# Where and on which engine an attention-plus-MLP kernel forms the operands of its seven-product blocks

## The chip, the cores and the metric

The kernel runs on one core of a Trainium2 chip. The metric is the device time of one execution in microseconds (us), as the median of several runs. The core has five engines with a queue each: TensorE (PE: matmuls, and PEld: their weight loads), VectorE (DVE), ScalarE (ACT), GpSimd (POOL) and SyncE (SP), which here issues nearly all DMAs. Each engine takes its instructions in the order of its queue; an instruction that waits holds all behind it on the same engine.

## The reference

Attention over chunks, then a gated MLP on its output:

```
for each chunk c of 32 queries (768 queries, 4 batches, 8 heads of 64):
    keys = 8 memory keys + the chunk with 16 to its left and 8 to its right
    a    = softmax(q_c @ keys.T / 8)
    out  = a @ values
x  = out as 3072 tokens x 512
xn = x / sqrt(mean(x*x) + 1e-6) * rms_g
g, val = xn @ w_gate, xn @ w_val            # 512 x 1536 each
y  = (silu(g) * val) @ w_out                # 1536 x 512
```

## The kernel before

The 3072 tokens are eight blocks of 384. A block's MLP goes over twelve column groups f of 128 of the 1536 columns. Every float32 operand is held as a high part in the matmul format (`fp32r`) and a remainder, and a product is three matmuls: high by high, high by remainder, remainder by high (`PASS`).

**Stages in the order of time.** The first and second block run first, with the loading and splitting of the weights, in an order written out by hand (`ORDER`); of the first block the column groups 5 to 11 are left over. Then `segments` runs the first block's rest, the third block (`blk` 2) and the fourth block (`blk` 3, its column groups in the order 10, 11, 0 to 9). For each column group TensorE does the gate product (`pg`, 12 matmuls), the value product (`pv`, 12) and, one column group behind, the output product (`po`, 9); ScalarE and VectorE do the silu between them (tanh L478, L482, L485, the high part `hh` L173, the remainder `hl` L494). There is one PSUM buffer each for `pg` and `pv`. In the first block VectorE has one multiply more per column group (L473, into the tile `gr`).

The last four blocks run in two pairs (`whole`). There the gate and value products of two blocks and two column groups are formed from seven products in place of eight (`CHAIN`), from sums and differences of weights and of activations, and the parts are added up by VectorE (`products`).

**The weights' sums and differences (the operands of the seven products).** `keep(w, p)` (L766) makes them for one weight matrix (`g` or `v`) and one pair of column groups: SyncE stores the weights that are used as they are (L770, L771) into DRAM; GpSimd adds high part and remainder of both column groups into a tile `ks` (L775, two operations of 128x512) and makes four sums and differences in it (L777, 128x256 each); ScalarE casts the result to the high part in the tile `late["tmp"]` (L779, shown as `qp`); VectorE subtracts to leave the remainder in `ks` (L780); SyncE stores both (L782). `keep_o(f)` (L757) stores the output weights of one column group. There is one tile `ks` and one for the high part. The list `keeping` holds 24 such calls; `visit` (L940) makes the next of them at gaps of the third and fourth block: those of the third whose number does not leave 3 on division by 4, and the odd ones from 1 to 11 of the fourth. A gap is the place behind a `pg` (even numbers) or a `pv` (odd numbers), so a block has 24. Nothing but data and buffers ties these calls to their place: the program's planner orders every engine's queue by a simulated time, and only matmuls are held in program order there.

**Attention.** The attention of the third to eighth block is cut into steps (`late_steps`): "p" transposes, "s" scores and softmax, "o" output, "n" the three parts of the normalization (`late_n`; L348, L349 and L353 are its last operations). `VISITS` says at which gaps of a segment which steps come, `SUPER` does so for the seven-product stage of the first pair. At the end of a block `split_x` (L733) makes high part and remainder of the next block's activations, and the last silu (L747, L748).

**The activations' sums.** `x_first`, `x_second` and `x_rest` make the activations' sums and differences for the seven products by `half` (cast and remainder, L815 and L816) and `minus` (L819), each on 128x768. For the first pair they come behind column groups number 7 and 10 of the fourth block and at its end. The first 30 loads of stored operands (`load(NR)`, L811) are issued behind column group number 7 of the fourth block.

## Time and profile before

| | us |
|---|---|
| median of 3 runs | 707.48 |
| lowest and highest run | 705.79 and 708.33 |
| the profiled execution's own time | 708.44 |
| its span, first to last instruction | 706.7 |
| TensorE busy | 672.8 |
| VectorE busy | 449.5 |
| ScalarE busy | 299.2 |
| GpSimd busy | 75.0 |

Mean granted TensorE clock: 0.983 of full speed. The third block's first gate product starts at about 227 us, the fourth's at 317 and the first seven-product at about 410.

The rows of the trace give a start time or a total in us, the engine and the line, the operation with its output and inputs by their names in the program, their shapes, and how often it stands there. In square brackets or behind an arrow stands how long the engine was idle just before and what it was waiting for. The name of a tile is the name under which its buffer was first made: `qp` is also `late["tmp"]`.

### The profile page before, as it was taken

The page shows a single profiled execution, that of the slowest core. Times are in us where ns is not written, and L with a number is a line of the kernel's source. Part 1 is how long each engine was busy: PE and PEld are TensorE (multiplying, and loading weights), DVE is VectorE, ACT ScalarE, POOL GpSimd, SP SyncE. Part 2 cuts the span into 40 slices and gives each one's busy share as a digit, 9 for nine tenths or more (in the row PEclk, how much of TensorE's full clock was granted, in tenths as well). Part 3 has the DMA queues.
Part 4 walks back from the last instruction along what each step waited for, and adds up shares of the span by engine and source line. Part 5 has one row for each costly group of instructions (what it writes and reads, how often), then busy time and mean ns, then how long its engine had stood idle before and what let it go on. Part 6 is the DMA issues. An engine that isn't in the chain of part 4 may idle for free.

```text
span 706.7 us, 15057 instructions
## 1 busy us (share of the span) xinstructions
PE 672.8 (95%) x6134; PEld 613.5 (87%) x6134; DVE 449.5 (64%) x831; ACT 299.2 (42%) x516; POOL 75.0 (11%) x84
## 2 busy tenths in 40 slices
PE   7899999999886989999999999999999999999997
PEld 6797888999775988799999989989988899999885
DVE  6689988887587543585585967569729254455221
ACT  4597867843333331433324254343424343332112
POOL 0010000034536335300000000000000000000000
PEclk8799999999998999999999999999999999999999
DMA  9659997866642252513319668896733598885002
GB/s 328 266 164 338 313 342 245 268 221 224 223 165 102 93 185 68 182 58 135 105 46 355 256 206 248 298 304 222 251 113 120 165 304 252 254 251 176 0 1 89
DMA packets 79700, 140.18 MB, mean 198 GB/s; under 512 B 7440, under 2 KB 33040, under 8 KB 79632
## 3 DMA queue, kind: packets, MB, share of 16 engines
q1 hardware_dynamic: 77760, 136.08, 58.0%
q10 hardware_dynamic: 1872, 3.15, 1.2%
q8 instruction: 48, 0.79, 0.4%
q14 instruction: 20, 0.16, 0.1%
HBM read 104.60 MB, written 34.60 MB: 197 GB/s over the span
## 4 chain that ended last, share of the span: by engine, by line
PE 65%; DVE 10%; DMA 9%; POOL 7%; ACT 6%; issue 3%; SPq 0%; POOLq 0%; DVEq 0%; ACTq 0%
PE po L915 14%; PE mga L886 7%; PE mva L886 7%; PE pg L464 6%; PE po L514 6%; PE pv L464 6%; POOL ks L777 4%; POOL ks L775 3%; PE mve L886 3%; PE mge L886 3%; DMA ws<-in_moe_w_out_dram 2%; DMA kv<-ks 2%; PE mvc L886 2%; PE mgc L886 2%; DVE ks L780 2%
## 5 line engine op out<-in xcount | busy, mean ns | idle before, releaser
L915 PE MATMUL po<-r,hhs 128*128 128x512 f32 x288 | 90.5, 395 | 0.0
L464 PE MATMUL pv<-xh,wh_v 128*128 128x384 f32 x192 | 66.2, 345 | 7.8 <-ACT xT L316 4.7
L464 PE MATMUL pg<-xh,wh_g 128*128 128x384 f32 x192 | 68.0, 354 | 3.4 <-DVE t L482 2.1
L464 PE MATMUL pv<-xh,wl_v 128*128 128x384 f32 x192 | 65.7, 342 | 0.5 <-DVE wl_v L435 0.5
L464 PE MATMUL pg<-xl,wh_g 128*128 128x384 f32 x192 | 65.9, 343 | 0.0
L464 PE MATMUL pg<-xh,wl_g 128*128 128x384 f32 x192 | 65.8, 342 | 0.0
L464 PE MATMUL pv<-xl,wh_v 128*128 128x384 f32 x192 | 65.5, 341 | 0.0
L514 PE MATMUL po<-wh_o,hh 128*128 128x512 f32 x144 | 58.8, 408 | 6.4 <-ACT hh L747 5.4
L915 PEld LDWEIGHTS po<-r,hhs 128*128 128x128 f32 x288 | 54.1, 188 | 12.3
L514 PE MATMUL po<-wh_o,hl 128*128 128x512 f32 x144 | 58.2, 404 | 1.1 <-DVE hl L494 1.1
L886 PE MATMUL mga<-x,r 128*128 128x384 f32 x288 | 58.4, 338 | 0.0
L886 PE MATMUL mva<-x,r 128*128 128x384 f32 x288 | 58.1, 337 | 0.0
L514 PE MATMUL po<-wl_o,hh 128*128 128x512 f32 x144 | 57.6, 400 | 0.0
L915 PE MATMUL po<-r,hls 128*128 128x512 f32 x144 | 56.8, 395 | 0.0
L897 DVE TENSOR_TENSOR hls<-h,hhs 128x768 fp32r<-128x768 f32 x24 | 22.9, 956 | 45.3 <-ACT hhs L896 45.3
L886 PEld LDWEIGHTS mga<-x,r 128*128 128x128 f32 x288 | 50.4, 188 | 1.0 <-ACT e L858 0.6
L886 PEld LDWEIGHTS mva<-x,r 128*128 128x128 f32 x288 | 50.5, 188 | 0.1
L896 ACT CAST hhs<-h 128x768 fp32r<-128x768 f32 x24 | 20.0, 835 | 68.1 <-PE po L915 64.1
L464 PEld LDWEIGHTS pv<-xh,wh_v 128*128 128x128 f32 x192 | 36.4, 190 | 10.2 <-ACT xT L316 5.6
L173 ACT CAST hh<-t 128x384 fp32r<-128x384 f32 x46 | 23.7, 516 | 46.3 <-PE po L514 22.2
L464 PEld LDWEIGHTS pg<-xh,wh_g 128*128 128x128 f32 x192 | 36.8, 192 | 6.7 <-DVE t L482 2.6
L777 POOL TENSOR_TENSOR ks<-ks 128x256 f32<-128x256 f32 x48 | 37.9, 789 | 2.8
(154 smaller groups left out, 1461.3 us busy)
## 6 DMA issues: line engine op xcount, KB each, us to landing
r<-kg SPq DMA_DIRECT2D x84, 256.0 KB, 3.3
r<-kv SPq DMA_DIRECT2D x84, 256.0 KB, 3.3
r<-ko SPq DMA_DIRECT2D x48, 256.0 KB, 3.1
kv<-in_v_dram SPq DMA_DIRECT2D x24, 384.0 KB, 4.8
kv<-in_k_dram SPq DMA_DIRECT2D x24, 312.0 KB, 3.8
ws<-in_moe_w_gate_dram SPq DMA_DIRECT2D x4, 1024.0 KB, 7.1
ws<-in_moe_w_val_dram SPq DMA_DIRECT2D x4, 1024.0 KB, 7.2
ws<-in_moe_w_out_dram SPq DMA_DIRECT2D x4, 1024.0 KB, 7.1
```

The costliest lines, as they stand in the source:

```text
L173: return nc.scalar.copy(out, in_)
L464: on_pe(nc.tensor.matmul(ps[:, 0:HT], lhsT=weight(a, n, f, kt), rhs=xs[c][:, kt], start=kt == 0 and i == 0, stop=kt == NKT - 1 and i == 2))
L514: on_pe(nc.tensor.matmul(po[i], lhsT=h[a][:, i * P:(i + 1) * P], rhs=weight(c, "o", f), start=f == first and n == 0, stop=f == end and n = ...
L775: nc.gpsimd.tensor_tensor(out=s[:, i:i + 2], in0=h, in1=l, op=ALU.add)
L777: nc.gpsimd.tensor_tensor(out=s[:, o], in0=s[:, a], in1=s[:, b], op=op)
L780: nc.vector.tensor_tensor(out=s.bitcast(F32R), in0=s, in1=h.bitcast(F32), op=ALU.subtract)
L886: on_pe(nc.tensor.matmul(bank[w, b], lhsT=r[:, a, kt], rhs=x[:, c, kt], start=bool(first) and kt == 0 and i == 0, stop=kt == 1 and i == 2, ...
L896: nc.scalar.copy(hh, sup["h", f])
L897: nc.vector.tensor_tensor(out=hl, in0=sup["h", f], in1=hh.bitcast(F32), op=ALU.subtract)
L915: on_pe(nc.tensor.matmul(po[i], lhsT=cur[a][:, i * P:(i + 1) * P], rhs=r[c], start=f == n == 0, stop=f == NF - 1 and n == 2))
```

## The change

The sums and differences of the weights are formed in three steps at set gaps, for each of twelve items (a weight matrix and a pair of column groups), 36 gaps in all: every gap of the third block and the first twelve of the fourth. An item's steps are:

1. VectorE makes the four sums and differences (before: GpSimd), and GpSimd's two sums for the next item are issued;
2. ScalarE casts the high part, in two halves, into a tile of its own (`kh`);
3. VectorE makes the remainder, in two halves, and SyncE issues all of the item's stores, those of one column group of the output weights among them.

GpSimd's two sums for the first item are issued at gap 11 of the first block. `tc.issue_after` holds each step behind what VectorE and ScalarE were given before it. The summed tile has two buffers in turn (`ks` and `late["tmp"]`). `rb0`, `rb1` and `gr` become parts of one tile, whose place is used by `kh` later and by `spare` in the seven-product stage. The attention visits of the fourth block come two gaps sooner, and those in the seven-product stage move. `x_second` comes one column group sooner, and `half` and `minus` work in two halves.

```diff
-          3: {3: "ps", 3.5: "o", 7: "ps", 7.5: "o", 9: "n", 10: "n", 11: "n",
-              13: "ps", 13.5: "o", 17: "ps", 17.5: "o", 19: "n", 20: "n", 21: "n"}}
+          3: {1: "ps", 1.5: "o", 5: "ps", 5.5: "o", 7: "n", 8: "n", 9: "n",
+              11: "ps", 11.5: "o", 15: "ps", 15.5: "o", 17: "n", 18: "n", 19: "n"}}
...
-SUPER = {("A", 1, 2): "p", ("A", 1, 6): "s", ("A", 1, 11): "o", ("A", 2, 11): "p", ("A", 3, 2): "s", ("A", 3, 7): "o",
-         ("A", 3, 12): "n", ("A", 4, 2): "n", ("A", 4, 6): "n", ("A", 4, 10): "p", ("A", 4, 13): "s", ("A", 5, 5): "o",
-         ("B", 1, 5): "p", ("B", 2, 5): "o", ("B", 3, 5): "n", ("B", 4, 2): "n", ("B", 4, 5): "n"}
+SUPER = {("A", 1, 1): "p", ("A", 1, 4): "s", ("A", 2, 0): "o", ("A", 3, 0): "p", ("A", 3, 3): "s", ("A", 4, 0): "o",
+         ("A", 4, 3): "n", ("A", 4, 6): "n", ("A", 5, 1): "n", ("A", 5, 2): "p", ("A", 5, 5): "s", ("B", 0, 2): "o",
+         ("B", 2, 2): "p", ("B", 3, 2): "o", ("B", 4, 2): "n", ("B", 4, 5): "n", ("B", 5, 2): "n"}
...
-        t = p1.tile([P, HT], F32, name="gr", tag="gr")
+        t = gr
...
-    rb = [p1.tile([P, HT], F32, name=f"rb{i}", tag=f"rb{i}") for i in range(2)]
+    spare = p1.tile([P, 3, HT], F32, name="rg", tag="rg")
+    rb, gr = [spare[:, i] for i in range(2)], spare[:, 2]
...
+    def dump(f, w, cols, to):
+        k, i, n = fgroup[f]
         for part in range(2):
-            nc.sync.dma_start(out=t[:, part], in_=weight_all(part, "o", f).bitcast(F32))
+            c = wt[part, w, k].bitcast(F32)[:, i * DM:(i + 1) * DM]
+            nc.sync.dma_start(out=to[:, :, part], in_=c[:, cols].rearrange("p (k f) -> p k f", k=to.shape[1]))
+
+    items, sums = [(p, w) for p in (5, 0, 1, 2, 3, 4) for w in "gv"], {}
+
+    def keep_load(k):
+        p, w = items[k]
+        s = sums[k] = (late["tmp"] if k % 2 else p1.tile([P, 2 * DM], F32, name="ks", tag="wy")).rearrange("p (k f) -> p k f", k=4)
+        for i, f in enumerate(reversed(PAIRS[p])):
+            c, n, _ = fgroup[f]
+            h, l = (wt[part, w, c][:, n * DM:(n + 1) * DM].bitcast(F32).rearrange("p (k f) -> p k f", k=2) for part in range(2))
+            nc.gpsimd.tensor_tensor(out=s[:, 2 * i:2 * i + 2], in0=h, in1=l, op=ALU.add)
+
+    def keep(g):
+        k = g // 3
+        if k >= len(items):
+            return
+        p, w = items[k]
+        s = sums[k]
+        with ExitStack() as behind:
+            for eng in (nc.vector, nc.scalar):
+                behind.enter_context(tc.issue_after(last_of(eng)))
+            if g % 3 == 0:
+                for o, a, b, op in ((1, 0, 1, ALU.add), (0, 2, 0, ALU.subtract), (2, 1, 2, ALU.subtract), (3, 3, 2, ALU.subtract)):
+                    nc.vector.tensor_tensor(out=s[:, o], in0=s[:, a], in1=s[:, b], op=op)
+                if k + 1 < len(items):
+                    keep_load(k + 1)
+            elif g % 3 == 1:
+                sums["h"] = h = p1.tile([P, 3 * HT], F32R, name="kh", tag="rg")[:, 0:2 * DM].rearrange("p (k f) -> p k f", k=4)
+                for i in range(2):
+                    nc.scalar.copy(h[:, 2 * i:2 * i + 2], s[:, 2 * i:2 * i + 2])
+            else:
+                h, t = sums["h"], dram.tile([P, 7, 2, DM // 2], F32, name=f"k{w}{p}")
+                l = s.bitcast(F32R)
+                for i in range(2):
+                    c = slice(2 * i, 2 * i + 2)
+                    nc.vector.tensor_tensor(out=l[:, c], in0=s[:, c], in1=h[:, c].bitcast(F32), op=ALU.subtract)
+                kept[w, p] = t
+                nc.sync.dma_start(out=t[:, 3:7, 0], in_=h.bitcast(F32))
+                behind.enter_context(tc.issue_after(last_of(nc.sync)))
+                nc.sync.dma_start(out=t[:, 3:7, 1], in_=s)
+                fa, fb = PAIRS[p]
+                dump(fa, w, slice(0, DM), t[:, 0:2])
+                dump(fb, w, slice(DM // 2, DM), t[:, 2:3])
+                f = fa if w == "g" else fb
+                kept["o", f] = t = dram.tile([P, 2, DM], F32, name=f"ko{f}")
+                dump(f, "o", slice(0, DM), t.unsqueeze(1))
...
     def half(t, src):
-        nc.scalar.copy(t[:, 0], src)
-        nc.vector.tensor_tensor(out=t[:, 1], in0=src, in1=t[:, 0].bitcast(F32), op=ALU.subtract)
+        for i in range(2):
+            nc.scalar.copy(t[:, 0, i], src[:, i])
+            nc.vector.tensor_tensor(out=t[:, 1, i], in0=src[:, i], in1=t[:, 0, i].bitcast(F32), op=ALU.subtract)
...
         def visit(gap):
+            if blk == 0 and gap == 11:
+                keep_load(0)
+            if blk and gap == int(gap):
+                keep(24 * (blk - 2) + gap)
             for c in VISITS[blk].get(gap, ""):
                 if next(todo) != c:
                     raise AssertionError(gap)
-            if blk == 2 and gap in range(24) and gap % 4 != 3 or blk == 3 and gap in range(1, 12, 2):
-                next(keeping)()
...
-                if blk == 3 and n == 10:
+                if blk == 3 and n == 9:
                     x_second(4)
...
-        sup["e", w, n] = lambda i=i: (p1 if i < 2 else sup["hpool"]).tile([P, HT], F32, name=f"e{i}", tag=f"rb{i}" if i < 2 else f"e{i}")
+        sup["e", w, n] = lambda i=i: sup["spare"][:, i] if i < 2 else sup["hpool"].tile([P, HT], F32, name=f"e{i}", tag=f"e{i}")
```

## The prediction

> **What bounds the kernel now.** I read the page's busy times and chain first, then a table of stretches, then TensorE's pauses one by one, then who held the engine that each pause names.

> ```profile
> PE 672.8 (95%) x6134; PEld 613.5 (87%) x6134; DVE 449.5 (64%) x831; ACT 299.2 (42%) x516; POOL 75.0 (11%) x84
> ...
> HBM read 104.60 MB, written 34.60 MB: 197 GB/s over the span
> ```

> TensorE is busy for 672.8 of 706.7 us: only the 34 us in which it stands, and the time in which it runs at a reduced clock, can be won. The question is how much of both lies where the change works. Columns of the next rows: PE, PEld, DVE, ACT, POOL busy, granted clock, DMA share, GB/s.

> ```profile
> 180.00:223.00 43.00, 32.86 (x364) 28.40 (x356) 34.54 (x63) 15.51 (x30) 19.47 (x20) 0.94 0.50 166
> 223.00:260.00 37.00, 36.95 (x360) 34.04 (x361) 18.30 (x34) 12.38 (x23) 16.97 (x18) 0.93 0.40 136
> 260.00:288.00 28.00, 25.47 (x134) 23.04 (x132) 10.89 (x17) 7.42 (x13) 11.19 (x13) 1.00 0.31 108
> 288.00:317.00 29.00, 27.57 (x314) 23.96 (x313) 21.57 (x47) 10.92 (x23) 5.61 (x6) 1.00 0.32 106
> 317.00:363.50 46.50, 46.50 (x606) 43.27 (x605) 28.18 (x65) 14.83 (x31) 0.00 (x0) 1.00 0.29 97
> 363.50:409.00 45.50, 44.56 (x586) 39.92 (x585) 34.24 (x74) 16.38 (x32) 0.00 (x0) 1.00 0.72 254
> ...
> 196.00:199.00 3.00, 1.75 (x7) 1.75 (x8) 1.47 (x3) 2.14 (x5) 0.00 (x0) 0.79 0.98 297
> 199.00:202.00 3.00, 3.00 (x12) 2.72 (x11) 2.33 (x6) 0.72 (x2) 2.67 (x2) 0.64 0.56 216
> 223.00:226.00 3.00, 2.95 (x7) 2.37 (x8) 2.97 (x4) 1.93 (x4) 1.62 (x2) 0.50 0.27 93
> 226.00:229.00 3.00, 3.00 (x11) 2.71 (x11) 0.09 (x1) 1.26 (x2) 2.84 (x4) 0.59 0.42 157
> ```

> The first stretch is the end of the first block, the third block runs from 223 to 317, the fourth from 317 to 409. Where POOL works (to 297), TensorE pauses; from 317 to 363.5 POOL is idle and TensorE does not pause at all. So the operands, which the code names only in the third and fourth block, are formed much earlier, in the first block's tail. The pauses:

> ```profile
> 184.19 0.44 PE L464 MATMUL pv<-xh,wh_v 128*128 128x384 f32 x1 [1.43 <-ACT xT L316]
> 187.17 0.87 PE L274 MATMUL pT<-ident,pe 128*128 128x128 f32 x6 [0.60 <-DVE gr L473]
> ...
> 197.25 0.44 PE L464 MATMUL pv<-xh,wh_v 128*128 128x384 f32 x1 [1.96 <-ACT xT L316]
> ...
> 208.92 0.50 PE L514 MATMUL po<-wh_o,hl 128*128 128x512 f32 x1 [0.58 <-DVE hl L494]
> 215.71 0.50 PE L514 MATMUL po<-wh_o,hl 128*128 128x512 f32 x1 [0.18 <-DVE hl L494]
> ...
> 223.05 0.79 PE L514 MATMUL po<-wh_o,hh 128*128 128x512 f32 x1 [5.45 <-ACT hh L747]
> ...
> 263.17 0.45 PE L464 MATMUL pg<-xh,wh_g 128*128 128x384 f32 x1 [2.14 <-DVE t L482]
> ...
> 296.73 0.44 PE L464 MATMUL pv<-xh,wh_v 128*128 128x384 f32 x1 [1.28 <-ACT xT L316]
> ...
> 407.22 0.50 PE L514 MATMUL po<-wh_o,hh 128*128 128x512 f32 x1 [0.93 <-ACT hh L173]
> ...
> 477.09 1.33 PE L886 MATMUL mve<-x,r 128*128 128x384 f32 x6 [1.62 <-DVE e L861]
> ```

> None names POOL. The link is one step back, in ScalarE's and VectorE's queues:

> ```profile
> ACT qp L779 <- POOL ks L777: 38.8, 10, 5.9
> ```
> ```profile
> 260.35 1.05 ACT L779 CAST qp<-ks 128x1024 fp32r<-128x1024 f32 x1 [5.32 <-POOL ks L777]
> 261.30 0.48 ACT L478 ACTIVATE t<-pg 128x384 f32<-128x384 f32 x1
> ```
> ```profile
> 211.86 2.77 DVE L348 SCALAR_TENSOR_TENSOR rq<-rq,rt 128x384 f32<-128x384 f32 x2
> 214.55 1.10 DVE L494 TENSOR_TENSOR hl<-t,hh 128x384 fp32r<-128x384 f32 x1
> 215.57 1.08 DVE L349 SCALAR_TENSOR_TENSOR rr<-rq,rr 128x384 f32<-128x384 f32 x1
> 216.69 3.03 DVE L353 SCALAR_TENSOR_TENSOR xT<-xT,rg,rr 128x384 f32<-128x384 f32 x4
> ...
> 220.12 1.21 DVE L780 TENSOR_TENSOR ks<-ks,qp 128x1024 fp32r<-128x1024 f32 x1
> ```
> ```profile
> 358.97 1.14 DVE L348 SCALAR_TENSOR_TENSOR rq<-rq,rt 128x384 f32<-128x384 f32 x2
> 360.15 0.56 DVE L349 SCALAR_TENSOR_TENSOR rr<-rq,rr 128x384 f32<-128x384 f32 x1
> ...
> 361.38 2.20 DVE L353 SCALAR_TENSOR_TENSOR xT<-xT,rg,rr 128x384 f32<-128x384 f32 x4
> ```
> ```profile
> 211.29 2.93 POOL L775 TENSOR_TENSOR ks<-wh_v,wl_v 128x512 f32<-128x512 f32 x2 [5.70 <-DMA kg<-ks]
> ```

> First, the cast L779 stands at the head of ScalarE's queue until POOL has finished its six operations, 38.8 us in ten waits; the tanh behind it (261.30) is late, and TensorE stands 2.14 us at 263.17. Second, VectorE is slower beside POOL: the pair L348 took 2.77 us under POOL's two sums against 1.14 alone, L349 1.08 against 0.56, the four L353 3.03 against 2.20. Third, the cast's remainder L780 stands in the same queue.

> **The change, part by part.**

> *The first block's tail.* All but the first item's sums move behind the third block's start. The pauses from 180 to 223.05 add up to 1.43 + 0.60 + 1.96 + 0.58 + 0.18 + 5.45 = 10.2 us. What of the 5.45 is inherent? Taking out what is named above: 1.63 (L348) + 0.5 (hl, about half of 1.10) + 0.52 (L349) + 0.83 (L353) + 1.21 (L780) = 4.7, which leaves 0.7; more if VectorE has other work to catch up, as this block has one multiply more per column group (L473) than the third. I put 1.0 back, with bounds 0 and 5.45.

> *The clock.* Behind the pauses at 197 and 223 the granted clock fell. Loss: 1.75 x (1 - 0.79) + 3 x (1 - 0.64) = 1.5 us, and 2.95 x (1 - 0.50) + 3 x (1 - 0.59) = 2.7 us; together 4.2, which goes with the pauses. [...] So I charge new pauses up to 2.7 us, and 0.5 as the likeliest.

> *The third block's inside.* 2.14 and 1.28 us are ScalarE's cast waiting for POOL; with the differences made a step earlier by another engine they go: 3.4. The price is VectorE's:

> ```profile
> L780 DVE TENSOR_TENSOR ks<-ks,qp 128x1024 fp32r<-128x1024 f32 x12 | 14.7, 1223 | 25.4 <-ACT qp L779 25.4
> ...
> L321 DVE TENSOR_TENSOR sq<-sq,sq 128x384 f32<-128x384 f32 x18 | 10.0, 558 | 11.0 <-ACT sq L319 10.2
> ```

> No row shows a 128x256 operation on VectorE. From 384 elements (558 ns) to 1024 (1223 ns) it is 1.04 ns an element, so about 425 ns (below the 558 row, above its proportional 372); four, overlapping as the L353 do, about 1.5 us. The remainder, now two halves, stays about 1.25. Each of twelve items thus holds VectorE for 2.75 us where it held it 1.22, and POOL's two sums slow it by 1 us (bounds 0 and the 2.93 of the sums' own length). [...]

> A new wait comes with it: the differences wait at the head of VectorE's queue for POOL's sums, with silu, hl and attention behind them, and TensorE behind those. The sums are issued one item ahead and have a second buffer, so I cost this wait at nothing in the third block. What decides is the landing of the store that frees the buffer, against the length of a gap:

> ```profile
> 304.33 2.11 PE pv L464 x12
> 306.44 2.10 PE po L514 x9
> ```
> ```profile
> 248.11 6.07 DMA kv<-ks
> ...
> 274.29 3.19 DMA kv<-ks
> ```

> A column group (pg like pv, then po) takes 6.3 us, a gap half of that. Four gaps, 12.6 us, lie between the remainder and the differences that reuse its buffer. The remainder (1.25), two issues (about 1), the landing (3.2 alone, 6.1 beside the attention's loads) and the sums (2.9) need 8.4 to 11.3. It holds, with 1.3 us to spare at the worst. ScalarE's cast has one buffer: two gaps, 6.3 us, between the store of its high part and the next cast, against 3.2 to 6.1; it holds too, barely at the worst, and the tanh stands behind it. On SP's queue the stores now lie among the attention's loads, which are needed a visit (four gaps or more) later; the products' first 30 operand loads come behind the fourth block's eighth column group and read items stored by then. Both at nothing.

> *The third block's end.* Seven gaps from 288 to 317 get three remainders and two sets of differences: 6.75, plus 2 for POOL, minus 1.2 for the L780 in it now. VectorE: 21.6 + 7.5 = 29.1 us in 29 - 1.4 = 27.6 us of TensorE's time. It overflows by 1.5, and part of its idle time can't be used (it waits for TensorE's results), so I take a pause of 3 us ahead of the fourth block; bounds 0 and 6.

> *The fourth block's first twelve gaps.* The attention two gaps sooner brings both pairs and the whole normalization into them: this is the work of the stretch 317 to 363.5, 28.2 us of VectorE, to be done in about 45. Four items add 4 x 3.75 = 15: 43.2 of 45, 96%. I take pauses of 2 us in all, bounds 0 and 8.

> *What gets sooner behind them.* At 407.22 the cast waits behind the products' own sums; two gaps (some 6 us) more ahead of it remove 0.93. At 477.09 (1.62) the later attention's steps move too, but VectorE's load there stays what it is: I leave it, bounds 0 and 3.2. The splitting of casts and differences into halves adds a start to each, off TensorE's path.

> *The sum*, in the profiled execution: 706.7 - 10.2 - 4.2 - 3.4 - 0.9 = 688.0; + 1.0 + 0.5 + 3 + 2 = 694.5. Its time was 708.44 for a span of 706.7, 1.7 above, and the median of the runs lies 1.0 below it: 694.5 + 0.7 = **695 us**.

> **The rivals.**

> *VectorE is the bound.* Every sum of POOL's costs VectorE its full length: 12 x 1.9 = 23 us more of VectorE's time, of which the two full stretches (some seven items) can hide nothing: 13 us, about half of it given back by the attention's slack: 701 to 706. For it: 96% without that. [...]

> *Slower: the differences wait for the sums.* The stores are 28 of the 34.6 MB written (the output is 3072 x 512 x 4 bytes, 6.3 MB), and the 36 gaps from 223 to 363 give them some 130 us: 215 GB/s, beside the attention's loads. If the landing rises by over 1.3 us above the 6.1, each item stalls VectorE as ScalarE is stalled now. Then today's pauses and clock loss (10.2 + 4.2 + 3.4 = 17.8) come back on an engine with more behind it, beside my 6.5: 695 + 18 = 713. For it: 6.07 at 248.11. Against: the stores stand first in each item's burst.

> *The pauses of the first block are its own.* The normalization's chain ends just before the block does. Then 8 of the 14.4 us stay: 703. Against: the third block ends with the same visits and no pause of its own at 317.

> *Everything fits.* No new pause: 694.5 - 6.5 + 0.7 = 689; with 477.09 gone 687.

> **How the numbers follow.** Chances: forecast 0.60 (own range 690 to 701), VectorE the bound 0.13, the differences' wait 0.11, the first block's own pauses 0.09, everything fits 0.07. The range 688 to 705 leaves out the slower case, most of the last one, and the ends of the others. A measurement tells 0.3%, 2.1 us: faster is below 705.4: 0.60 + 0.07 + 0.08 + 0.09 = 0.84; within 0.3% some 0.05 from VectorE as the bound; slower 0.11.

> **What would show it.** Right: no L780-like remainder and no POOL work between 155 and 210; no pause above 1.5 us and clock 1.00 at the first block's end; POOL at about half of its 75.0 us; VectorE above 90% in the fourth block's first half, with pauses there naming hl or t. Wrong: VectorE's differences waiting microseconds for POOL's sums, a pause above 2 us that still stands ahead of the third block, or clock dips behind pauses in the fourth.

## The result, and the profile after

The changed kernel takes 700.59 us (median of 4 runs, 699.07 to 701.63) against 707.9: a ratio of 0.9899, 95% interval 0.9868 to 0.9929. It is faster, by 7.3 us where 12.5 were forecast. The profiled execution took 699.07 us, and its span is 697.1 against 706.7.

Busy times of the page, after, then stretches of the trace (columns: PE, PEld, DVE, ACT, POOL busy, granted clock, DMA share, GB/s):

```profile
PE 668.8 (96%) x6134; PEld 610.5 (88%) x6134; DVE 471.4 (68%) x913; ACT 301.5 (43%) x542; POOL 38.5 (6%) x36
```
```profile
155.00:196.00 41.00, 41.00 (x665) 37.73 (x664) 28.56 (x74) 14.39 (x31) 0.00 (x0) 1.00 0.41 135
196.00:210.00 14.00, 14.00 (x71) 12.35 (x71) 11.08 (x24) 7.14 (x14) 0.00 (x0) 1.00 0.16 57
210.00:299.00 89.00, 82.98 (x779) 74.54 (x778) 68.52 (x132) 29.01 (x59) 20.54 (x14) 1.00 0.67 230
299.00:345.00 46.00, 42.20 (x563) 38.24 (x562) 32.54 (x74) 16.04 (x34) 7.55 (x6) 0.93 0.88 298
345.00:400.00 55.00, 53.01 (x628) 47.30 (x628) 42.42 (x97) 19.50 (x41) 0.00 (x0) 1.00 0.72 254
```

The first two rows are the first block's tail: POOL has no work in it, and TensorE does not pause. The stretch from 299 to 345 us, in the fourth block, has the lowest clock, the busiest DMA, and a TensorE that stands for 3.8 us. TensorE's pauses of 0.3 us and more in the third and fourth block:

```profile
222.29 0.88 PE L274 MATMUL pT<-ident,pe 128*128 128x128 f32 x6 [0.61 <-DVE t L482]
...
231.86 0.45 PE L464 MATMUL pv<-xh,wh_v 128*128 128x384 f32 x1 [0.94 <-ACT xT L316]
...
275.14 0.44 PE L464 MATMUL pv<-xh,wh_v 128*128 128x384 f32 x1 [0.89 <-ACT xT L316]
...
295.64 0.51 PE L514 MATMUL po<-wh_o,hh 128*128 128x512 f32 x1 [2.37 <-ACT hh L748]
296.97 0.50 PE L514 MATMUL po<-wh_o,hl 128*128 128x512 f32 x1 [0.60 <-DVE hl L749]
309.26 0.31 PE L305 MATMUL oe<-kv,kv 64*64 64x32 f32 x1 [2.75 <-issue]
331.94 0.44 PE L464 MATMUL pv<-xh,wh_v 128*128 128x384 f32 x1 [0.91 <-ACT xT L316]
...
349.58 0.88 PE L274 MATMUL pT<-ident,pe 128*128 128x128 f32 x6 [1.61 <-DVE t L482]
398.42 0.50 PE L514 MATMUL po<-wh_o,hh 128*128 128x512 f32 x1 [0.37 <-ACT hh L173]
```
```profile
307.00:310.00 3.00, 0.74 (x6) 0.68 (x7) 1.62 (x2) 0.00 (x0) 2.48 (x2) 0.76 0.98 327
310.00:313.00 3.00, 3.00 (x11) 3.00 (x11) 2.99 (x9) 1.38 (x4) 0.00 (x0) 0.50 0.71 238
313.00:316.00 3.00, 3.00 (x12) 2.85 (x11) 2.95 (x11) 1.72 (x5) 0.00 (x0) 0.60 1.01 319
```

Behind the pause of 2.75 us the clock fell; the last three rows, busy time by missing share of the clock, give 0.74 x 0.24 + 3 x 0.5 + 3 x 0.4 = 2.9 us lost. "Issue" says that TensorE waited for nothing that the profile shows.

Where the gain came from and went is read by counting TensorE's matmuls in both traces and taking the start of the same one (times in us; between 2790 and 4010 the change moves attention steps, so no mark is taken there):

| matmul number | before | after | lead | won in the stretch | forecast |
|---|---|---|---|---|---|
| 950 | 90.88 | 88.88 | 2.0 | 2.0 | 0 |
| 1100 | 123.26 | 117.86 | 5.4 | 3.4 | 0 |
| 2100 (16 us into the third block) | 243.24 | 223.13 | 20.1 | 14.7 | 13.4 |
| 2790 (ahead of the third block's last silu) | 313.99 | 292.40 | 21.6 | 1.5 | 3.4 |
| 4010 (just behind the fourth block) | 412.49 | 403.55 | 8.9 | -12.6 | -4.6 |
| 6100 (near the end) | 694.11 | 684.60 | 9.5 | 0.6 | 0 |

So the lead was 21.6 us, and more than half of it was given back in one stretch of 110 us.

### The profile page after: what moved, and what is told of

Same layout as the page of the kernel before. It is cut to its first block, busy times and chain, and to the rows that moved or that the text cites. A ratio compares the mean times of both kernels' runs of the same rounds, so it can differ in the third digit from the quotient of the medians.

```text
span 697.1 us, 15110 instructions
## 1 busy us (share of the span) xinstructions
PE 668.8 (96%) x6134; PEld 610.5 (88%) x6134; DVE 471.4 (68%) x913; ACT 301.5 (43%) x542; POOL 38.5 (6%) x36
## 3 DMA queue, kind: packets, MB, share of 16 engines
HBM read 104.60 MB, written 34.60 MB: 200 GB/s over the span
## 4 chain that ended last, share of the span: by engine, by line
PE 84%; DVE 8%; ACT 5%; issue 2%; DMA 1%; SPq 0%; ACTq 0%; DVEq 0%
PE po L937 14%; PE pg L464 12%; PE po L514 12%; PE pv L464 12%; PE mga L908 7%; PE mva L908 7%; PE mve L908 4%; PE mge L908 4%; PE s L211 2%; PE mvc L908 2%; PE pT L274 2%; PE mgc L908 2%; PE oe L305 2%; PE ss L625 1%; ACT ws L419 1%
## 5 line engine op out<-in xcount | busy, mean ns | idle before, releaser
L464 PE MATMUL pv<-xh,wh_v 128*128 128x384 f32 x192 | 66.1, 344 | 4.0 <-ACT xT L316 2.7
L464 PE MATMUL pg<-xh,wh_g 128*128 128x384 f32 x192 | 67.7, 352 | 0.0
L464 PE MATMUL pg<-xl,wh_g 128*128 128x384 f32 x192 | 66.3, 345 | 0.5 <-DVE xl L649 0.5
L464 PE MATMUL pg<-xh,wl_g 128*128 128x384 f32 x192 | 66.2, 345 | 0.0
L464 PE MATMUL pv<-xh,wl_v 128*128 128x384 f32 x192 | 65.2, 340 | 0.5 <-DVE wl_v L435 0.5
L464 PE MATMUL pv<-xl,wh_v 128*128 128x384 f32 x192 | 65.4, 340 | 0.0
L514 PE MATMUL po<-wh_o,hh 128*128 128x512 f32 x144 | 58.1, 403 | 2.7 <-ACT hh L748 2.4
L514 PE MATMUL po<-wh_o,hl 128*128 128x512 f32 x144 | 57.2, 397 | 0.6 <-DVE hl L749 0.6
L514 PE MATMUL po<-wl_o,hh 128*128 128x512 f32 x144 | 56.9, 395 | 0.0
L173 ACT CAST hh<-t 128x384 fp32r<-128x384 f32 x46 | 23.8, 518 | 52.5 <-PE po L514 43.2
L494 DVE TENSOR_TENSOR hl<-t,hh 128x384 fp32r<-128x384 f32 x46 | 29.3, 637 | 19.9 <-ACT hh L173 19.8
L464 PEld LDWEIGHTS pv<-xh,wh_v 128*128 128x128 f32 x192 | 36.5, 190 | 6.1 <-ACT xT L316 3.7
L464 PEld LDWEIGHTS pg<-xl,wh_g 128*128 128x128 f32 x192 | 37.0, 193 | 2.1 <-DVE xl L649 0.7
```

What stands on the lines that cost most here:

```text
L173: return nc.scalar.copy(out, in_)
L464: on_pe(nc.tensor.matmul(ps[:, 0:HT], lhsT=weight(a, n, f, kt), rhs=xs[c][:, kt], start=kt == 0 and i == 0, stop=kt == NKT - 1 and i == 2))
L494: nc.vector.tensor_tensor(out=hl, in0=t, in1=hh.bitcast(F32), op=ALU.subtract)
L514: on_pe(nc.tensor.matmul(po[i], lhsT=h[a][:, i * P:(i + 1) * P], rhs=weight(c, "o", f), start=f == first and n == 0, stop=f == end and n = ...
```

## The experiments

Two questions were open: which part of the change brings the lead, and what takes it back. For the first, theory P held that it is the place (the sums out of the first block's tail) and theory E that it is the engine (no wait of ScalarE for six operations of GpSimd); theories S (the three steps) and U (the second buffer) came when both had fallen. For the second the theories are D, V, B, F, N, Q and R, named in the expectations. The median of the kernel before differs by up to 1 us from one set of runs to the next, so the ratios to the kernel before that ran beside each are compared:

| kernel | median us | ratio | 95% interval |
|---|---|---|---|
| after | 700.59 | 0.9899 | 0.9868 to 0.9929 |
| place_only | 712.96 | 1.0066 | 1.0043 to 1.0090 |
| engine_only | 714.36 | 1.0082 | 1.0058 to 1.0107 |
| steps_pool | 702.63 | 0.9922 | 0.9904 to 0.9939 |
| old_visits | 701.62 | 0.9908 | 0.9873 to 0.9942 |
| one_burst | 699.76 | 0.9874 | 0.9849 to 0.9899 |
| one_buffer | 719.36 | 1.0145 | 1.0119 to 1.0171 |
| o_later | 703.98 | 0.9939 | 0.9920 to 0.9958 |
| raw_early | 704.72 | 0.9947 | 0.9927 to 0.9967 |
| stores_free | 698.86 | 0.9866 | 0.9835 to 0.9898 |
| fetch_shift | 699.04 | 0.9865 | 0.9841 to 0.9889 |
| tail_free | 697.04 | 0.9829 | 0.9799 to 0.9859 |
| tail_shift | 687.87 | 0.9715 | 0.9683 to 0.9748 |

### Which part brings the lead

**place_only.** The kernel before, each `keep` call (and each `keep_o` in the same way) held behind what VectorE and ScalarE were given ahead of its gap:

```diff
     def keep(w, p):
+        with ExitStack() as behind:
+            for eng in (nc.vector, nc.scalar):
+                behind.enter_context(tc.issue_after(last_of(eng)))
+            keep_all(w, p)
...
```

> The kernel before, with one thing added: each of the 24 calls that form or store operands is held behind what VectorE and ScalarE were given before its gap, so that it can't run ahead into the first block. GpSimd still makes all six operations of an item, and there is one buffer. Theory P (place): the gain of the change is the first block's tail (pauses of 10.2 us and a clock loss of 4.2 us before), so it comes here too, less what ScalarE's waits for GpSimd then cost in the third and fourth block (3.4 us before for six items, up to 8 for twelve): 698 to 703 us, and no pause over 1 us ahead of the third block. Theory E (engine): the gain is that ScalarE no longer waits for GpSimd's four differences; nothing of that is in this kernel, so the pauses only move: 706 to 710.

The first block's tail is free of pauses, as P said: from 115.1 to 244 us there is none of 0.3 us or more. But pauses of 15.8 us now stand in the third and fourth block, such as

```profile
247.53 0.50 PE L514 MATMUL po<-wh_o,hh 128*128 128x512 f32 x1 [3.06 <-ACT hh L173]
...
308.84 0.50 PE L514 MATMUL po<-wh_o,hh 128*128 128x512 f32 x1 [2.73 <-ACT hh L747]
...
332.92 0.44 PE L464 MATMUL pv<-xh,wh_v 128*128 128x384 f32 x1 [2.79 <-ACT xT L316]
```

and TensorE's busy time rose to 677.1 us, with a lower clock. At its set place, with one buffer, the work costs more than in the tail; the time lies above what either theory gave.

**engine_only.** The kernel before, the four differences (L777) by VectorE:

```diff
-            nc.gpsimd.tensor_tensor(out=s[:, o], in0=s[:, a], in1=s[:, b], op=op)
+            nc.vector.tensor_tensor(out=s[:, o], in0=s[:, a], in1=s[:, b], op=op)
```

> The kernel before, with the four differences of an item on VectorE in place of GpSimd; place, buffers and calls as before. Theory P: the items still run in the first block's tail, on a VectorE that is 34.5 of 43 us busy there; ScalarE's waits shrink by the 3.2 us that GpSimd needs for the differences, but the work ahead of the third block does not: most of the 14 us stays, 703 to 708. Theory E: ScalarE's 38.8 us of waiting nearly go and the pauses with them: 696 to 701, as the whole change or better.

Slower by 0.8%: the longest pauses of TensorE are 4.18, 3.80 and 6.11 us. The wait has moved from ScalarE to VectorE, which holds silu and attention behind it (VectorE's waits from 120 to 420 us):

```profile
DVE ks L777 <- POOL ks L775: 16.8, 10, 3.4
```

E alone is a loss, and P's 703 to 708 is missed too.

**steps_pool.** The kernel after, the four differences (L785) by GpSimd again (the same line of code, changed the other way).

> The changed kernel, with the four differences back on GpSimd, in the same three steps at the same gaps with the same two buffers. Theory P: the first block's tail stays clear; VectorE has 18 us less to do in the third and fourth block, GpSimd 35 us more beside it, and a cast can wait for GpSimd: within 4 us of the changed kernel, 697 to 704. Theory E: ScalarE waits for GpSimd again at each item, as before the change: 706 to 712.

P's numbers held: POOL is busy for 80.5 us, yet the ratio lies within the interval of the kernel after. One of these operations takes GpSimd 789 to 903 ns on the mean, against VectorE's 0.41 us; where the sums lie ready early enough, that costs nothing that can be measured.

**old_visits.** The kernel after with `VISITS`, `SUPER` and the place of `x_second` as before.

> The changed kernel, with the attention's visits of the fourth block and of the seven-product stage, and the place of x_second, as they were before. Theory D (transfers): the pause of 2.75 us without a releaser at 306.5, and the clock loss of some 2.9 us behind it, come from scores and output matmuls standing back to back behind the fourth block's first value product, while the stores fill the DMA engines; visits two gaps later put an output product between them, so both go, and the 0.93 and 1.62 us of before come back: 697 us, with pauses of about 3 us left at the end of the third block. Theory V (VectorE): the fourth block's pauses come from VectorE's load; a normalization two gaps later relieves it too, so every pause from 300 to 360 goes, not only this one: 693 to 695. If neither holds, the pause moves to another place: 700.

0.9908 against 0.9899: the sooner visits are worth nothing that can be measured, and neither D's 697 nor V's 693 to 695 came. Its fourth block has no "issue" pause above 0.34 us, but others: 2.29, 0.93 and 1.58 us ahead of attention's transposes and 1.61 + 1.01 at 398, where the kernel after has 0.37.

**one_burst** and **one_buffer.** The kernel after with an item's three steps at one gap, and the kernel after with one buffer for the sums, filled behind the third step:

```diff
-                keep(24 * (blk - 2) + gap)
+                g = 24 * (blk - 2) + gap
+                for i in range(g - 2, g + 1) if g % 3 == 2 else ():
+                    keep(i)
```
```diff
-        s = sums[k] = (late["tmp"] if k % 2 else p1.tile([P, 2 * DM], F32, name="ks", tag="wy")).rearrange(...)
+        s = sums[k] = p1.tile([P, 2 * DM], F32, name="ks", tag="wy").rearrange(...)
...
-                if k + 1 < len(items):
-                    keep_load(k + 1)
...
+                if k + 1 < len(items):
+                    keep_load(k + 1)
```

> The kernel after, with the three steps of an item on one gap (its third) and two buffers as they are: what is left of the change is the second buffer, VectorE for the differences, the place and the sooner visits. Theory S (the split into steps carries the gain): VectorE is held some 4 us at a time, 1.5 for the differences, 1.2 for the cast that it waits for and 1.3 for the subtraction, and attention's and the experts' operations queue behind it: pauses of 10 us and more in the third and fourth block, 706 to 710. Theory U (the second buffer carries it): the sums lie ready, so nothing is waited for but the cast: pauses as in the kernel after within 3 us, 700 to 703.

> The kernel after, with one buffer for the sums, filled again once the subtraction of the item ahead is stored; the three steps as they are. Each filling then waits for a landing (3.3 us, up to 5.9 in a full DMA) and takes 2.5 us, against one gap of some 4 us until the differences want it: VectorE would wait 2 to 4 us with each of 11 items, and hold what is queued behind it. Theory U (the second buffer carries the gain): pauses of 10 us and more in the third and fourth block, 706 to 712. Theory S (the steps carry it): what VectorE waits for is short enough to be hidden: 700 to 704.

U has the sign right in both and S in neither; the sizes are off, one_burst a little below U's 700 to 703 and one_buffer 7 us above its 706 to 712. The waits of VectorE from 205 to 400 us show it (what waited and for what: total, times, longest), first of one_buffer, then of the kernel after:

```profile
DVE ks L785 <- POOL ks L772: 18.2, 7, 4.4
```
```profile
DVE qp L785 <- POOL qp L772: 2.1, 1, 2.1
```

In one_burst this wait does not occur at all. One buffer alone makes 0.9899 to 1.0145, some 18 us. At the new place the second buffer is what makes the change a gain; for the steps, the engine and the visits the intervals overlap with that of the kernel after. A second buffer at the old place was not tried, so whether the place is needed beside it stays open; nor were the halves in `half` and `minus` tried alone.

### What takes it back

**o_later** and **raw_early.** The pause at 309.26 stands where the fourth block's first visit puts attention's scores and its output products back to back, 96 small matmuls each, in 2.5 us. In o_later the first "o" comes at gap 3.5 in place of 1.5. In raw_early the plain weights are stored at the first block's gaps 0 to 11, to relieve the queue:

```diff
-          3: {1: "ps", 1.5: "o", 5: "ps", 5.5: "o", 7: "n", 8: "n", 9: "n",
+          3: {1: "ps", 3.5: "o", 5: "ps", 5.5: "o", 7: "n", 8: "n", 9: "n",
```
```diff
+            if blk == 0 and gap in range(12):
+                keep_raw(gap)
...
```

> The changed kernel, with one step moved: the attention's first output step of the fourth block at gap 3.5 in place of 1.5, so that an output product of the MLP stands between its scores and its output matmuls. VectorE's work before it is the same, the stores too. Theory D: the pause of 2.75 us without a releaser goes, and the clock loss with it: 700.6 - 5.6 = 695 us. Theory V: what stands in the way is VectorE waiting for GpSimd's sums (2.09 us at 308.4) and its load: the pause moves by a column group and stays in size, 699 to 702.

> The changed kernel, with part of the stores moved: the weights that are stored as they are (768 KB of each item's 2.36 MB) are stored at the first block's gaps 0 to 11, where the DMA engines are 0.3 to 0.4 busy, in place of the third step of each item. Theory D: the DMA engines are no longer full at 297 to 316, so the store that frees GpSimd's buffer lands sooner, VectorE's wait of 2.09 us and TensorE's pause of 2.75 us go or shrink to under 1 us, and the clock keeps up: 694 to 697 us; the first block may lose up to 2 us to the stores. Theory B (back to back alone): the two bursts of small matmuls are enough for the pause, whatever the DMA engines do: it stays at 2 to 3 us, 699 to 702. Theory V: the same, 699 to 702, with the pauses at the third block's end (2.37 and 0.60 us) unchanged under all.

In o_later that pause went and others came: 3.64 us behind VectorE at 319.51 and 1.11 "issue" at 334.51. In raw_early VectorE's wait for the sums fell from 2.09 to 1.15 us and the pause grew to 3.51 us at the same instruction; two waits for attention loads (0.83 and 1.86 us) came in the first block. The DMA engines were as full around the pause as without the edit (0.99 busy from 305 to 313 us, against 0.90), so raw_early did not take away what theory D names, and says nothing against it. Neither is a gain: both ratios are 0.4 to 0.5% above that of the kernel after, with intervals that just touch its own.

**fetch_shift.** A window of DMA, 306.8 to 307.9 us of the kernel after, shows inside the pause one packet of a queue of the kind "instruction", which has 48 on the page:

```profile
q8 instruction: 48, 0.79, 0.5%
```

Theory F takes these for the packets of TensorE's own instructions: 6134 weight loads, 6134 matmuls and 180 others are 12,448 entries, 259 for each of 48 packets of 16 KB. Counted from the start, the "issue" pauses of the kernel after (26.00, 227.72, 270.92, 309.26) stand at the entries 962, 4545, 5314 and 6081: all 193 or 194 above a multiple of 256. The packet in the last pause lands at 307.81, and TensorE goes on 1.45 us later (1.3 in steps_pool and raw_early). The test moves the packets against the work:

```diff
-    warm(22)
+    warm(13)
```

> The kernel after, with 9 of the 22 warming matmuls at the very start left out, so that every later TensorE instruction stands 36 places earlier in its list (each of them is four entries); nothing else. Theory F: the pause of 2.75 us at 309.26 comes from TensorE's instructions being fetched in packets of 256; in the traces so far each pause that waits for nothing (26.00, 227.72, 270.92, 309.26 of the kernel after) stands at entry 193 or 194 of a packet, and at 309 two packet ends lie in a run of small matmuls 1.6 us long. Moved by 36 entries, one of the two falls among the large products ahead of it, which leave time for the next packet. F expects that pause under 0.3 us, the clock behind it at 1.00 (2.9 us), and so 695 to 698 against 700.6, about 0.993 of it. Theory N: the pause belongs to scores and output products standing back to back, whatever the packets; it stays between 2 and 3.6 us at the same instruction, and the time at 700 to 702.

F is right on the mechanism: the pauses at 26 and 309 are gone, and the two that are left stand again at the entries 4545 and 5314 of the shifted list, that is, at other instructions.

```profile
226.06 0.25 PE L305 MATMUL oe<-kv,kv 64*64 64x32 f32 x2 [0.52 <-issue]
...
268.56 0.19 PE L305 MATMUL oe<-kv,kv 64*64 64x32 f32 x1 [0.18 <-issue]
...
293.36 0.80 PE L514 MATMUL po<-wh_o,hh 128*128 128x512 f32 x1 [2.90 <-ACT hh L748]
312.09 0.44 PE L464 MATMUL pv<-xh,wh_v 128*128 128x384 f32 x1 [3.60 <-ACT xT L316]
```

F is wrong on the price: TensorE ran on and then stood 3.60 us for ScalarE's copy of `xT`, which is behind VectorE's softmax. VectorE and GpSimd in that place:

```profile
304.68 3.46 DVE L797 TENSOR_TENSOR ks<-ks,kh 128x512 fp32r<-128x512 f32 x2
308.07 0.41 DVE L785 TENSOR_TENSOR qp<-qp 128x256 f32<-128x256 f32 x1
308.40 1.01 DVE L222 TENSOR_REDUCE mx<-s 128x6 f32<-128x384 f32 x2
```
```profile
304.22 3.38 POOL L772 TENSOR_TENSOR qp<-wh_v,wl_v 128x512 f32<-128x512 f32 x2 [16.39 <-DVE kv L176]
```

The two halves of the remainder took 3.46 us beside GpSimd's sums; in the kernel after they took 1.28 at 305.01, and VectorE then waited for the sums. Either way the softmax comes late: at 308.40 here, at 309.77 in the kernel after. Two causes stood one behind the other, and taking away the first uncovers the second.

How long the pause lasts goes with the DMA engines. The two microseconds from entry 5825 on, in the kernel after, raw_early and stores_free (columns as above, the DMA share last but one; packets count where they start, so it can pass 1):

```profile
304.40:306.40 2.00, 2.00 (x152) 1.91 (x137) 1.85 (x4) 0.10 (x1) 0.00 (x0) 1.00 1.04 346
307.25:309.25 2.00, 2.00 (x153) 1.91 (x138) 1.87 (x4) 0.11 (x1) 0.78 (x1) 1.00 1.02 343
309.00:311.00 2.00, 2.00 (x154) 1.91 (x143) 1.96 (x5) 0.15 (x1) 0.00 (x0) 1.00 0.19 34
```

The next packet starts 2.5, 3.4 and 0.9 us behind that entry, and TensorE's pause at 6081 is 2.75, 3.51 and 1.22 us. The four other runs with this crossing fit: one_burst 1.22 us with the DMA 0.14 busy; steps_pool, one_buffer and tail_free 2.20, 2.29 and 2.19 us with 1.04 to 1.05. So F has the place of the pause, and its length goes with full DMA engines, as D had it; no run was made for that alone.

**tail_free.** The third block's 24 steps on its first 20 gaps:

```diff
-                keep(24 * (blk - 2) + gap)
+                a, b = (24 + gap, 25 + gap) if blk == 3 else (-(-6 * min(gap + i, 20) // 5) for i in range(2))
+                for g in range(a, b):
+                    keep(g)
```

> The kernel after, with the third block's 24 steps on its first 20 gaps (at gaps 0, 5, 10 and 15 two of them), its last four gaps free; the fourth block as it is. Theory Q: the 2.37 and 0.60 us that the output products wait at 295.64 and 296.97 come from item 7's four differences (1.6 us) and its subtraction (0.68) in VectorE's queue ahead of the last gate and of hl; without them the two are under 1.0 us together, and the wait of VectorE for the sums at 308.38 (2.09) goes with them, since item 7's stores go out some 5 us sooner: 697 to 699 with the clock. Rival R: attention's normalization, which keeps VectorE busy without a break from 285.7 to 294.5, is what makes the gate late, and the steps only use its remainder: the pauses stay at 2 us or more, 700 to 702, and the doubled gaps cost pauses of their own in the third block.

Q is right. The pauses of 2.37 and 0.60 us are gone, VectorE does not wait for the sums in the fourth block (it does once in the third, for 1.18 us at 263.72), and no slice of 3 us from 100 to 400 has a clock below 1.00. R has a small part: TensorE pauses for 1.18 us at 265.73, behind a doubled gap. Of the two causes at the fourth block's start, the fetch alone is left:

```profile
303.14 0.24 PE L305 MATMUL oe<-kv,kv 64*64 64x32 f32 x1 [2.19 <-issue]
```

**tail_shift.** Both edits together.

> The third block's last four gaps free of steps, together with the 9 warming matmuls less, which move TensorE's packets of instructions. The two were measured apart: 697.0 and 699.0 against 700.6. Where the moved packets were tried alone, the pause at 26 us (1.96) and the one at 309 went, but TensorE then stood 3.60 us for ScalarE's copy of xT, which is behind VectorE's softmax and that behind the wait for the sums. Theory F with that bound: with the steps out of the third block's end VectorE doesn't wait there, so both gains are had: 1.96 at the start and 0.8 at 303 (the copy of xT ends 1.2 us after the pause does there, and the next products wait for it): 693 to 695.5. Rival N: the copy of xT bounds that place in any case, and what is won at the start is lost before the third block: 696.5 to 698.

The ratio is 0.9715: some 20 us faster than the kernel before and about 2% faster than the one after. The two pauses of fetch_shift and tail_free at that place become one short one, and one behind a cast follows:

```profile
302.73 0.44 PE L464 MATMUL pv<-xh,wh_v 128*128 128x384 f32 x1 [1.40 <-ACT xT L316]
...
320.35 0.45 PE L464 MATMUL pv<-xh,wh_v 128*128 128x384 f32 x1 [1.04 <-ACT xT L316]
```

F had 693 to 695.5, so 5 us more were won than it can say. Its sum has no term for the clock, whose mean over all executions is 0.988 in tail_free and 0.993 in tail_shift: some 3.5 us of 690. The two profiled executions differ by 6.4 us in span: 1.5 at matmul 2100 and 3.5 at 4010, about what F says, and the rest in the seven-product stage, where tail_free has pauses that neither tail_shift nor the kernel after has:

```profile
471.67 1.32 PE L908 MATMUL mge<-x,r 128*128 128x384 f32 x6 [0.63 <-DVE e L883]
477.06 1.32 PE L908 MATMUL mve<-x,r 128*128 128x384 f32 x6 [1.98 <-DVE e L883]
```

Why these come and go was not found out.

**stores_free.** The lead of 5.4 us at matmul 1100 was in nobody's sum. In the kernel before the plain weight stores stand in SP's queue among the loads of the weights; after, one line holds them back:

```diff
-                behind.enter_context(tc.issue_after(last_of(nc.sync)))
```

> The kernel after without the one line that keeps an item's plain weight stores in SP's queue behind the store of its rounded sums; the stores then stand again between the loads of the weights, as in the kernel before, and all else stays. Theory H (the place of the plain stores is a gain of its own, which the prediction had not in its sum): from 80 to 120 us the DMA engines are over 0.8 busy again, against 0.47 and 0.32, ScalarE waits for weights, and the pauses of 1.08 and 1.20 us at 101 and 114 come back: 2.3 us there. In the fourth block each item has 3 MB less to store, so a wait for a buffer as at 308.38 (2.09) gets shorter. In all 701 to 704. Rival G (the loads of the weights are early enough in any order, and the two pauses went with the sums): no pause there, and 698 to 700 from the emptier queue of the fourth block.

H is right on the early part, and misses the total: 698.86 us, where it had 701 to 704. (An item stores 2.36 MB in all; the edit takes the plain 1.3 MB of them out of the fourth block, not 3.) From 100 to 120 us, stores_free, then the kernel after:

```profile
100.00:120.00 20.00, 17.80 (x81) 15.34 (x80) 16.30 (x23) 13.63 (x19) 0.00 (x0) 0.91 0.77 264
```
```profile
100.00:120.00 20.00, 20.00 (x104) 18.36 (x103) 18.75 (x28) 15.90 (x21) 0.00 (x0) 1.00 0.32 105
```

The DMA is 0.77 busy against 0.32, the clock falls to a mean of 0.91, and matmul 1100 starts at 122.71 in place of 117.86. But matmul 4010 starts at 404.05 against 403.55: with the plain stores out of the fourth block's queue, VectorE's wait for the sums does not occur there, and the pause at entry 6081 is 1.22 us, the DMA engines being 0.19 busy there, without a fall of the clock. Gain and price of this line are about equal, 4 to 5 us each, in the profiled executions, and the total cannot be told from that of the kernel after.

## Why the prediction was right, and where it was not

*The first block's tail and its clock.* Right: no pause, clock 1.00, and no GpSimd work from 155 to 210 us; 14.7 us won against 13.4. place_only shows that the place does this. The pause of 5.45 left nothing at its place, where 1.0 had been put back.

*The third block's inside.* 1.5 us won in place of 3.4: ScalarE's wait for GpSimd went, but its cast now waits for VectorE's differences, and attention's copy of `xT` is still queued behind it. So TensorE stands for 0.94 and 0.89 us; the second:

```profile
273.71 0.62 ACT L791 CAST kh<-ks 128x512 fp32r<-128x512 f32 x1 [0.59 <-DVE ks L785]
274.23 0.47 ACT L316 COPY xT<-oe 128x384 f32<-128x384 f32 x1
```

The prediction had these waits go because the differences are made a step earlier; that came true in part only.

*The third block's end.* Right in size and cause: 3 us forecast, 2.37 + 0.60 measured, and tail_free takes them away by moving the steps.

*The fourth block's first twelve gaps.* The largest miss: 2 us of pauses and 0.5 of clock were forecast, 5.4 and 2.9 measured. The twelve gaps now lie between 299 and 355 us:

```profile
299.00:355.00 56.00, 50.59 (x773) 45.38 (x773) 42.35 (x95) 19.49 (x41) 7.55 (x6) 0.94 0.78 261
345.00:355.00 10.00, 8.39 (x212) 7.14 (x213) 9.81 (x22) 3.45 (x7) 0.00 (x0) 1.00 0.28 92
```

VectorE's work in them is as forecast, 42.35 us for 43.2 (the 1 us in each item for GpSimd's sums beside VectorE was the author's estimate, and no run shows it; in fetch_shift the two halves of L797 took 3.46 us beside the sums against 1.28 alone), and so is the one pause that hangs on its load: 1.61 us at 349.58 for 2, where VectorE is busy for 9.81 of 10 us. But the gaps took 56 us and not 45 (5.4 of pauses, 2.9 of clock, the rest work of TensorE's), so the load is 76% and not 96%. The step that failed is that VectorE alone would make the pauses there. The one of 0.91 us is again the copy of `xT` behind the cast. The largest, 2.75 us with the clock behind it, comes from the fetch of TensorE's own instructions (it is gone in fetch_shift, which moves their list by 36 entries), which was not in the prediction at all. Behind it stands a wait that the prediction named and costed at nothing. The stores of item 7 left SP's queue late, since its third step slipped behind `split_x`, and landed in 5.9 us in a full DMA, so that VectorE stood 2.09 us for GpSimd's sums:

```profile
308.38 1.47 DVE L785 TENSOR_TENSOR qp<-qp 128x256 f32<-128x256 f32 x1 [2.09 <-POOL qp L772]
```

The worst case had been worked out with 1.3 us to spare; it held for eleven items, and the slip used it up for one. Both signs named for "wrong" (a wait of microseconds for the sums, a fall of the clock in the fourth) did come, once each.

*What was missing.* The stores that leave the early part of SP's queue. The prediction asked of this queue what the moved stores run into, and not what they leave: 3.4 us between the marks 950 and 1100. The 2.0 us before that are the clock's: up to the mark 950 it was low for 13.7 us in the trace before and for 6.8 in the trace after. The difference is worth 3.4 us at half speed, less 1.2 us that the kernel after stands longer. Over the fourteen traces this early time lies between 3.4 and 13.7 us, so nothing shows that the change has a part in it.

*The rivals.* "The differences wait for the sums" is the mechanism that decides, one buffer short of the change: one_buffer took 719 us, where 713 was worked out for it. "VectorE is the bound" has every sum of GpSimd's cost VectorE its full length; two operations, L222 and L234, take 0.55 us beside the sums (L222 at 164.83 in the kernel before, L234 at 225.21 in the kernel after) as without them.

So the sign and the range were right; the forecast's gains fell short of the measured by 4.8 us and its prices by 8.0, and the one partly made up for the other, which is luck.

## What to carry to other kernels

When a producer is moved to fixed places, count its buffers first: here the second one decided between 1.5% slower and 1% faster, and the engine and the splitting, which looked like the change, did nothing measurable beside it at the new place. A work that leaves a queue is worth as much attention as the place that it goes to. When a pause names no releaser, count the entries of the engine's instruction list to it, see how full the DMA engines are there, and look for another wait close behind before pricing it.

## What the runs showed of the hardware

TensorE's pauses without a releaser stand a multiple of 256 entries apart: 193 or 194 above such a multiple in the kernel after, and again in fetch_shift, where every later instruction stands 36 entries sooner; 12,448 entries in 48 packets are 259 each. A run of small matmuls outran the packets there. Where it crossed two of these places within 1.9 us (entries 5825 and 6081 of the kernel after) TensorE stood 2.75 us; where 3.9 us lay between two (4289 and 4545), 0.23 us. It went on 1.3 to 1.5 us after the packet's landing. Of the first crossing, in a full DMA (1.04), 1.22 us were left where the DMA engines were 0.14 and 0.19 busy (one_burst, stores_free). The trace of the kernel after has 48 such places. At the 19 among products of 128x384 and 128x512 TensorE does not pause; of the 29 among smaller matmuls four have a pause: 1.96, 0.23, 0.22 and 2.75 us.

The two halves of L797 in fetch_shift, 3.46 us against 1.28 alone, end 0.54 us after the GpSimd sums beside them (308.14 against 307.60). The price was 2.2 us, between the 1 us that the prediction took and its bound of 2.9.
